# One core, attention and two expert layers: the first expert's first 128 slots are computed while the last token block is still at its gates

## The chip, the cores and the metric

The kernel runs on one core of a Trainium2 chip. The metric is the device time of one execution in microseconds, given as the median of several runs. Engines are named as in the profile: PE (TensorE matmul), PEld (its weight loads), DVE (VectorE), ACT (ScalarE), POOL (GpSimd), and SP, whose queue issues most DMAs. A trace of one execution gives all durations below.

## The reference

Three layers follow one another, on 2304 tokens (4 batches of 576) of 512 features:

```
attn = softmax(top-32 mask(q k^T / 8)) v            # 8 heads of 64, 576 tokens
h    = x @ w_in ; g = h * clip(h + 3, 0, 6) / 6      # w_in [512, 2048]
y    = g @ w_out                                     # w_out [2048, 512]
e    = argmax(y @ w_gate) ; gw = softmax(y @ w_gate)[e]   # 8 experts
out  = gw * (relu(y @ w1[e]) @ w2[e])                # w1 [8, 512, 1024], w2 [8, 1024, 512]
```

Each token passes exactly one of the eight experts. With the given inputs the experts get 328, 333, 249, 289, 285, 189, 284 and 347 tokens; the kernel has room for 384 of each (3 tiles of 128 slots).

## The kernel before, in words

All large products are made of float32r parts: each operand is split into a high part (a rounded copy) and a low part (the rest), and three matmuls (high by high, low by high, high by low) stand for one.

**First layer, in blocks.** The tokens go through the dense layer in 9 blocks of 256 (`NBLK`), each block in 16 steps of 128 hidden features. One step is 12 matmuls of 128x256 into `l1ps` (`l1`, L778), the clipped gate on ACT, DVE and POOL (`epi_a` L784, `epi_b` L790 which writes `gf`, `epi_c` L246 and L798 which write `gh` and `gl`), and 6 matmuls of 128x512 into `yps` (`l2`, L809). `l1ps` has two halves, so the next step but one can't start its first product before DVE has written `gf`. `moe_step` issues a step's pieces, and a scheduler with priorities orders each engine's instructions; what counts below is the order that comes out.

**The gates.** After a block's sixteenth step, `yevac` (L816) copies `yps` to SBUF, and `gate` runs once for each 128 tokens: four transposes, logits (L837), maximum, index and one-hot row (L848 to L860), the place of each token among those of its expert by matmuls with a triangle and with ones (L861, L862), the gate weight (L865), the write of the tokens to `yd` in DRAM (L866, SP) and the scatter of token numbers into the slot table `td` in DRAM (L887, POOL). For blocks 0 to 7 this goes on in the shade of the next block's steps. For the last block there is nothing left to shade it. Its tokens don't go through the table in DRAM: one-hot products add them (`placed`, L1079) to what was read back.

**The slot table.** `load_table` (L903, SP) reads the two tables that blocks 0 to 7 filled, `trow` (L904, DVE) takes the smaller of each pair, `tps` (L1077 to L1079) adds the last block's, and `tabg` (L1080) is the list that the gathers use.

**The experts.** `xgather` fetches the rows of `yd` for one expert (three indirect DMAs of 128 rows, L1092, POOL), `xprep` transposes and splits them (L1101 PE, L1103 ACT, L1104 DVE, and the gate weight `gw` L1105 POOL). Then for each of eight hidden pieces f of the expert come 12 matmuls of 128x384 (`m2l1`, `lp`, L1119), the split of the rectified result (L1123, L1124), and two pieces later 9 matmuls of 128x512 (`m2l2`, `ops`, L1136); `m2out` scales by the gate weight and scatters rows to the output. `wpiece` loads (L916, L919, SP) and splits (L926 ACT, L927 DVE) the expert weights, eight pieces for each expert; six pieces of expert 0 and the first two of expert 1 are split before the last block ends, and expert 0's other two after it.

Of the kernel before, what the change touches and what calls it, by code (L numbers as in the profile page):

```python
# [45 lines left out]
STEP = 400  # L46
# [8 lines left out]
def attention_two_moe_kernel(  # L55
# [139 lines left out]
    def body(cs, exact):  # L195
# [624 lines left out]
        def gate(bk, tt, y):  # L820
            pr("gate")
            i = bk * (TB // P) + tt
            last = bk == NBLK - 1
            yt = (wp[0] if last else m1p).tile([P, NCC, P], F32, tag="yt", bufs=1 + last, name=f"yt{i}")
# [19 lines left out]
            ad = (wp[0] if last else m1p).tile([P, 1], I32, tag="ad", bufs=2, name=f"ad{i}")  # L844
# [28 lines left out]
            if last:  # L873

                ad2 = m1p.tile([P, 1], I32, tag="ad2", bufs=2, name=f"ad2{i}")
                place, in128 = [wp[0].tile([P, n], F32, tag=f"oh{n}", bufs=2, name=f"oh{n}_{i}") for n in (P, NSL)]
                V.tensor_scalar(ad2, ad, P - 1, None, op0=ALU.bitwise_and)
                V.tensor_copy(sc[:, 4:5], ad2)
                V.tensor_tensor(sc[:, 5:6], sc[:, 3:4], sc[:, 4:5], op=ALU.subtract)
                V.tensor_scalar(place, cs["row"], sc[:, 4:5], None, op0=ALU.is_equal)  # L880
                V.tensor_tensor(sc[:, 6:7], cs["tokm"][:, i:i + 1], sc[:, 3:4], op=ALU.subtract)
                V.tensor_scalar(in128, cs["first"].rearrange("p e s -> p (e s)"), sc[:, 5:6], sc[:, 6:7],
                                op0=ALU.is_equal, op1=ALU.mult)
                placed.append((place, in128))

            def to_table():
                G.indirect_dma_start(td[tt], bass.IndirectOffsetOnAxis(ad, 0), tok[:, i:i + 1], None)  # L887

            if last:

                tables.append(to_table)
            else:
                to_table()
            gdone[0] += 1


        NSL = NE * SLOTS
        placed, gdone, trows, tables = [], [0], [], []
# [13 lines left out]
        def wpiece(e, i):  # L912
# [8 lines left out]
            late = kind and pc >= NPC // 2  # L921
            nb = 3 if kind else 5
            pool = tabp[0] if late else wp[0]
            h = pool.tile([P, 4 * FW], F32R, tag=f"wh{kind}", bufs=nb, name=f"wh{e}_{i}")
            l = pool.tile([P, 4 * FW], F32R, tag=f"wl{kind}", bufs=nb, name=f"wl{e}_{i}")
# [9 lines left out]
        def moe_step():  # L935
            g = gpos[0]
            if g >= NG + 3 or (g < NG and blkready[0] <= g // NF1):
                return
            gpos[0] += 1
            if 0 <= g - 1 < NG:  # L940
                epi_a(g - 1)
            yield
            if g >= 3:
                l2(g - 3)
                bk, f = divmod(g - 3, NF1)
                if f == NF1 - 1:
# [108 lines left out]
        pre = []  # L1055
        while gpos[0] < NG + 3 or pend:
            pr0[0] += STEP
            run(moe_step())
            gate_step()
            tc.cur_priority = pr0[0] + STEP  # L1060
            if gdone[0] == NTT - TB // P and not trows:
                load_table()
            if gpos[0] > NG - 12 and len(pre) < NPC + NPC // 2:

                pre.append(2 * len(pre) if len(pre) < NPC else 2 * (len(pre) - NPC) + 1)
                wpiece(0, pre[-1])
        m1.close()
        tc.cur_priority = pr0[0] + 2 * STEP


        tabp[0] = m2.enter_context(tc.tile_pool(name="tabp" + X, bufs=1))
        ps2 = m2.enter_context(tc.tile_pool(name="ps2" + X, bufs=1, space=PSUM))
        tab = tabp[0].tile([P, NSL], I32, name="tab")
        tabg = tabp[0].tile([P, NSL], I32, name="tabg")
        tps = ps2.tile([P, NSL], F32, tag="tp", bufs=2, name="tps")

# [4 lines left out]
        V.tensor_copy(tab, tps)  # L1081

        xst = {}

        def xgather(e):
# [3 lines left out]
            xg = []  # L1089
            for j in range(SLOTS):  # L1090
                x = tabp[0].tile([P, YW], F32, tag="xg", bufs=4, name=f"xg{e}_{j}")
                G.indirect_dma_start(x, None, yd, bass.IndirectOffsetOnAxis(tabg[:, e * SLOTS + j:e * SLOTS + j + 1], 0))  # L1092
                xg.append(x)
# [15 lines left out]
        def m2l1(e, f):  # L1109
# [6 lines left out]
            n = 0  # L1116
            for c in range(NCC):
                for a, b_ in ((h, xh), (h, xl), (l, xh)):
                    PE.matmul(lp, a[:, c, fs], b_[:, c, :], start=(n == 0), stop=(n == 3 * NCC - 1))  # L1119
# [3 lines left out]
            A.activation(hh, lp, AF.Relu)  # L1123
            V.scalar_tensor_tensor(hl, lp, 0.0, r_(hh), op0=ALU.max, op1=ALU.subtract)  # L1124
# [4 lines left out]
        def m2l2(e, f):  # L1129
# [3 lines left out]
            for j in range(SLOTS):  # L1133
# [4 lines left out]
        def m2out(e):  # L1138
            gw = xst[e][2]
            for j in range(SLOTS):  # L1140
                o = tabp[0].tile([P, DM], F32, tag="osb", bufs=3, name=f"osb{e}_{j}")
                A.activation(o, ops_[j], AF.Copy, scale=gw[:, j:j + 1])
                si = G.indirect_dma_start(out, bass.IndirectOffsetOnAxis(tab[:, e * SLOTS + j:e * SLOTS + j + 1], 0), o, None,
                                          bounds_check=NT - 1, oob_is_err=False)
                tc.declare_no_dep(si.ins, group="out" + X, reason="no token is in two slots")
                tc.add_to_no_dep_group("out" + X, si.ins)

        xgather(0)
        for f_ in tables:
            f_()  # L1150
        for i in range(2 * NPC):
            if i not in pre:
                wpiece(0, i)
        for j in range(SLOTS):
            xprep(0, j)
        seq = [(e, f) for e in range(NE) for f in range(NF2)]
        for s in range(len(seq) + 2):
            if s < len(seq):
                e, f = seq[s]
                if e + 1 < NE:  # L1160
                    if f == (e == 0):
# [9 lines left out]
            if s < len(seq) and e + 1 < NE:  # L1171
                wpiece(e + 1, f)
# [111 lines left out]
```

## Time and profile before

| | |
|---|---|
| median of 3 runs | 1294.11 us (1293.91 to 1296.38) |
| the profiled execution's own time | 1292.71 us |
| its span in the trace | 1290.9 us, 1.8 us less than its own time |
| PE busy | 1148.2 us, 89% of the span |
| DVE, ACT, POOL busy | 976.0, 821.9 and 345.8 us |
| mean granted PE clock | 0.957 of full speed |

Durations are taken from the profiled execution; its own time is 1.4 us below the median, so that a time worked out from it has 1.4 us added before it is compared with a median. The stretch that the change touches reaches from about 922 us (the last block's steps) to about 1039 us (the end of the first expert).

### The profile page before, as it was taken

How to read it: one execution, taken by the hardware profiler on the slowest of the kernel's cores; microseconds unless marked ns; L12 is line 12 of the kernel's file. 1: busy time of each engine (PE TensorE's matmuls, PEld its weight loads, DVE VectorE, ACT ScalarE, POOL GpSimd, SP SyncE). 2: the span in 40 equal slices, each digit the busy share in tenths (PEclk: the TensorE clock that was granted, in tenths of full speed). 3: DMA queues.
4: the chain of work that ended last, by engine and by line, in shares of the span. 5: the costliest groups of instructions: out<-in, count | busy, mean ns of one | idle time of the engine just before them, and what ended most of it. 6: DMA issues, size and time to landing. Idle time of an engine off the chain costs nothing.

```text
span 1290.9 us, 23533 instructions
## 1 busy us (share of the span) xinstructions
PE 1148.2 (89%) x7253; PEld 1017.9 (79%) x7253; DVE 976.0 (76%) x3882; ACT 821.9 (64%) x2087; POOL 345.8 (27%) x578
## 2 busy tenths in 40 slices
PE   4465688899999999999999999999975999999995
PEld 3354576788899788888788899898864999999994
DVE  5999999999999998998999999997422444444420
ACT  4777777788777777777777887786412444444421
POOL 2232255332332212222232322222334122212100
PEclk9987579899999999999999999999986999999998
DMA  5444466554644554544434544634774455555400
GB/s 141 134 123 143 119 201 214 162 144 130 151 121 120 137 161 119 153 125 124 119 105 125 158 124 129 147 115 118 265 210 108 142 162 169 164 156 168 133 19 26
DMA packets 184665, 180.21 MB, mean 140 GB/s; under 512 B 123933, under 2 KB 148813, under 8 KB 184528
## 3 DMA queue, kind: packets, MB, share of 16 engines
q1 hardware_dynamic: 180112, 167.52, 45.1%
q0 software_dynamic: 4416, 11.08, 2.9%
q8 instruction: 60, 0.98, 0.3%
q14 instruction: 77, 0.63, 0.2%
HBM read 160.52 MB, written 19.59 MB: 140 GB/s over the span
## 4 chain that ended last, share of the span: by engine, by line
PE 60%; DVE 9%; ACT 4%; DMA 3%; issue 2%; POOL 0%; SPq 0%; POOLq 0%; ACTq 0%; DVEq 0%
PE l1ps L778 11%; PE lp L1119 10%; PE ops L1136 10%; PE yps L809 10%; PE ptps L704 7%; PE sps L556 4%; PE ptps L670 3%; DVE pbuf L654 1%; DVE cd L586 1%; PE ptps L837 1%; DVE z L646 1%; PE tp L1101 1%; DVE z L619 1%; DVE cw L597 1%; PE misc L414 1%
## 5 line engine op out<-in xcount | busy, mean ns | idle before, releaser
L809 PE MATMUL yps<-wo,gh 128*128 128x512 f32 x576 | 209.6, 411 | 1.2 <-DMA wo<-wod 0.8
L778 PE MATMUL l1ps<-xh,wih 128*128 128x256 f32 x576 | 174.6, 303 | 15.2 <-DVE gf L790 10.4
L586 DVE MAX8 cd<-sbuf 128x8 f32<-128x72 f32 x1152 | 182.6, 220 | 2.0 <-ACT sbuf L248 1.9
L246 POOL TENSOR_SCALAR gh<-gf 128x256 fp32r<-128x256 f32 x144 | 64.3, 447 | 391.1 <-DVE gf L790 144.7
L778 PE MATMUL l1ps<-xh,wil 128*128 128x256 f32 x576 | 166.7, 289 | 0.0
L778 PE MATMUL l1ps<-xl,wih 128*128 128x256 f32 x576 | 166.4, 289 | 0.0
L927 DVE TENSOR_TENSOR wl<-raw,wh 128x1024 fp32r<-128x1024 f32 x64 | 79.4, 1243 | 96.3 <-ACT wh L926 94.3
L704 PE MATMUL ptps<-vn,pt 128*128 128x65 f32 (+1 forms) x1152 | 146.6, 282 | 0.0
L704 PEld LDWEIGHTS ptps<-vn,pt 128*128 128x128 f32 x1152 | 143.4, 201 | 0.0
L619 DVE SCALAR_TENSOR_TENSOR z<-sbuf,uall 128x576 f32<-128x576 f32 x144 | 132.7, 922 | 0.4 <-ACT uall L610 0.4
L778 PEld LDWEIGHTS l1ps<-xh,wih 128*128 128x128 f32 x576 | 112.1, 195 | 25.9 <-DVE gf L790 17.5
L654 DVE SCALAR_TENSOR_TENSOR pbuf<-sbuf,tall,pbuf 128x576 f32<-128x576 f32 x144 | 126.2, 877 | 0.1
L926 ACT ACTIVATE wh<-raw 128x1024 fp32r<-128x1024 f32 x64 | 67.7, 1060 | 85.2 <-PE lp L1119 40.3
L809 PEld LDWEIGHTS yps<-wo,gh 128*128 128x128 f32 x576 | 106.8, 191 | 16.9 <-issue 0.9
L784 ACT ACTIVATE gf<-l1ps,three 128x256 f32<-128x256 f32 x144 | 68.3, 474 | 78.4 <-PE l1ps L778 61.3
L670 PE MATMUL ptps<-ident,pbuf 128*128 128x128 f32 x576 | 97.9, 295 | 21.5 <-DVE j L650 14.9
L809 PE MATMUL yps<-wo,gl 128*128 128x512 f32 x288 | 116.3, 404 | 0.8 <-POOL gl L798 0.6
L248 ACT ACTIVATE sbuf<-sps 128x576 f32<-128x576 f32 x144 | 93.1, 647 | 37.2 <-PE sps L556 22.1
L798 POOL TENSOR_TENSOR gl<-gf,gh 128x256 fp32r<-128x256 f32 x144 | 112.5, 782 | 11.4
L627 ACT ACTIVATE pbuf<-sbuf,nb 128x576 f32<-128x576 f32 x144 | 111.2, 776 | 6.8 <-PE ptps L672 2.8
L636 ACT ACTIVATE jk<-sbuf,uall 128x576 bf16<-128x576 f32 x144 | 111.9, 777 | 3.2
L778 PEld LDWEIGHTS l1ps<-xl,wih 128*128 128x128 f32 x576 | 112.2, 195 | 1.8
(178 smaller groups left out, 2932.1 us busy)
## 6 DMA issues: line engine op xcount, KB each, us to landing
wo<-wod SPq DMA_DIRECT2D x144, 512.0 KB
raw<-in_moe_w_dram SPq DMA_DIRECT2D x64, 512.0 KB
vn<-in_v_dram SPq DMA_DIRECT2D x96, 128.0 KB
rawi<-in_moe_w_in_dram SPq DMA_DIRECT2D x16, 512.0 KB
rawo<-in_moe_w_out_dram SPq DMA_DIRECT2D x16, 512.0 KB
qn<-in_q_dram SPq DMA_DIRECT2D x128, 64.0 KB
wod<-wc SPq DMA_DIRECT2D x16, 512.0 KB
yd<-y SPq DMA_DIRECT2D x18, 258.0 KB
```

The costliest lines, as they stand in the source:

```text
L586: V.max(cd[:, c, :], s[:, c * CK:(c + 1) * CK])
L619: V.scalar_tensor_tensor(d["z"], s, d["u"], s, op0=ALU.is_le, op1=ALU.mult)
L627: A.activation(d["p"], d["s"], AF.Exp, bias=d["nb"], scale=SCALE)
L636: A.activation(jk, d["s"][:, 0:S], AF.Sign, bias=ts[t]["u"], scale=-1.0, accum_out=d["sg"])
L654: V.scalar_tensor_tensor(d["p"], d["s"], tall[:, t:t + 1], d["p"], op0=ALU.is_ge, op1=ALU.mult)
L670: PE.transpose(ptps[:, c * P:(c + 1) * P], pb[:, c0 + c * P:c0 + (c + 1) * P], ident)
L704: PE.matmul(d_, a_, b_, start=(i == 0), stop=(i == len(mm) - 1))
L778: PE.matmul(dst, a[:, c, fs], b_[:, c, :], start=(n == 0), stop=(n == 3 * NCC - 1))
L798: G.tensor_tensor(gl, gf, r_(gh), op=ALU.subtract)
L809: PE.matmul(yps[tt], a[:, tsl], b_, start=(f == 0 and m == 0), stop=(f == NF1 - 1 and m == 2))
L1119: PE.matmul(lp, a[:, c, fs], b_[:, c, :], start=(n == 0), stop=(n == 3 * NCC - 1))
L1136: PE.matmul(ops_[j], a[:, js], b_[:, ns], start=(f == 0 and m == 0), stop=(f == NF2 - 1 and m == 2))
```

## The change

**The early tile.** Expert 0's first 128 slots are filled by tokens of blocks 0 to 7 alone if these hold 128 tokens of expert 0. The changed kernel takes that for granted and checks it afterwards: `early_steps` transposes the slot table of blocks 0 to 7 (L1126), takes the token list (L1130, L1131), gathers those rows (`ex`, L1134, POOL) and transposes and splits them (L1139, L1142, L1143; the gate weight `egw` L1146 on POOL), all between steps of the last block. `early_products` runs both expert layers for these 128 slots: for each of eight pieces 12 matmuls of 128x128 (L1163) and 3 of 128x512 (L1176), placed behind the last block's products and among its gates. `early_out` scatters the result. A check (L1222, DVE) compares the early list with the final one and raises the flag that makes the kernel run again in another way; with 328 of the 2304 tokens in expert 0 it doesn't. Expert 0 then has two tiles left: its products are 128x256 instead of 128x384, and 6 instead of 9 of 128x512.

**The last block's gates.** `gate_last` does both halves of the last block at once: `yps` is evacuated on ACT and DVE at the same time (L894, L895), the eight transposes write back into `yps`, two copies (L905, L907) replace four, and `yd` is written in two parts (L898, L927). Its scatters into `td` move behind expert 1's gathers. The gates of other blocks take three pieces per step instead of one.

**The weights.** All eight pieces of expert 0 are loaded and split before the last block ends, and three pieces of expert 1 are loaded then too. Loading (`wload2`) and splitting (`wsplit`) are apart, and one piece is always loaded ahead.

**Expert 1's gathers** are held until the second hidden piece of expert 0 is done, by a copy from `hh` into the gather's tile (L1251).

```diff
+        def gate_last():
...
+            A.activation(ys[0][:, 0:DM], yps[0], AF.Copy, scale=1.0 / 6.0)
+            V.tensor_scalar(ys[1][:, 0:DM], yps[1], 1.0 / 6.0, None, op0=ALU.mult)
+            for tt in range(NTB):
+
+                SP.dma_start(yd[(i0 + tt) * P:(i0 + tt + 1) * P, 0:DM], ys[tt][:, 0:DM])
...
+        def early_steps():
+            tp = misc([P, 2, 2 * P])[:, 0, 0:NSL]
+            PE.matmul(tp, trows[0], ident[0:NSL, 0:NSL], start=True, stop=True)
...
+            x = m1p.tile([P, YW], F32, tag="ysb", bufs=2, name="ex0")
+            G.indirect_dma_start(x, None, yd[0:NT - TB, :], bass.IndirectOffsetOnAxis(tg, 0))
+            yield
+            yield
+            tp = ptps[:, 0:DM].rearrange("p (c n) -> p c n", c=NCC)
+            for c in range(NCC):
+                PE.transpose(tp[:, c, :], x[:, c * P:(c + 1) * P], ident)
...
+            for f in range(NF2 + 2):
+                if f < NF2:
...
+                            PE.matmul(lps[f % 2], a[:, c, fs], b_[:, c, :], start=(n == 0), stop=(n == 3 * NCC - 1))
...
+                if f >= 2:
...
+                        PE.matmul(op, a, b_[:, ns], start=(f2 == 0 and m == 0), stop=(f2 == NF2 - 1 and m == 2))
...
-            gate_step()
+            for _ in range(3):
+                gate_step()
...
-            for j in range(SLOTS):
+                if after is not None:
+
+                    G.tensor_copy(x[:, 0:1], after[:, CAP - 1:CAP])
+                    after = None
...
+            cols = slice(jfirst(e) * P, CAP)
...
-                    if f == (e == 0):
+                    if e == 0 and f == 2:
+                        xgather(1, r_(hst[0, 1][0]))
+                    elif e and f == 0:
                         xgather(e + 1)
```

Three places where the order of instructions changes follow; a number behind a name is a buffer's own and differs between the two kernels.

First DVE, in the last block's steps, where the smaller of the two tables (`trow`) is taken. Before:

```order
L790 SCALAR_TENSOR_TENSOR gf_13873<-gf_13873,l1ps 128x256
L790 SCALAR_TENSOR_TENSOR gf_13908<-gf_13908,l1ps 128x256
L927 TENSOR_TENSOR wl_0_14298<-raw_0_14295,wh_0_14297 128x1024
L790 SCALAR_TENSOR_TENSOR gf_13944<-gf_13944,l1ps 128x256
L869 SCALAR_TENSOR_TENSOR lex_13784,lsc_13783<-ptps,oh_13785 128x8
L872 CAST ad_13786<-lsc_13783 128x1
L790 SCALAR_TENSOR_TENSOR gf_13972<-gf_13972,l1ps 128x256
L927 TENSOR_TENSOR wl_1_14330<-raw_1_14327,wh_1_14329 128x1024
L904 TENSOR_TENSOR trow_14001<-trow_14001,trow_14002 24x128
L790 SCALAR_TENSOR_TENSOR gf_14006<-gf_14006,l1ps 128x256
L790 SCALAR_TENSOR_TENSOR gf_14033<-gf_14033,l1ps 128x256
```

After:

```order
L988 TENSOR_TENSOR wl_3_14047<-raw_3_13990,wh_3_14046 128x1024
L790 SCALAR_TENSOR_TENSOR gf_13795<-gf_13795,l1ps 128x256
L790 SCALAR_TENSOR_TENSOR gf_13829<-gf_13829,l1ps 128x256
L960 TENSOR_TENSOR trow_13784<-trow_13784,trow_13785 24x128
L790 SCALAR_TENSOR_TENSOR gf_13864<-gf_13864,l1ps 128x256
L1130 TENSOR_SCALAR etabg<-misc_13822 128x1
L1131 COPY ewas<-misc_13822 128x1
L988 TENSOR_TENSOR wl_5_14107<-raw_5_14050,wh_5_14106 128x1024
L790 SCALAR_TENSOR_TENSOR gf_13891<-gf_13891,l1ps 128x256
```

Before, the splits of expert 1's first two pieces (`wl_0`, `wl_1`) and the minimum `trow` stand between the block's `gf` results. After, expert 1's splits are not there; `trow` stands five `gf` further up in the block (nine follow it there, four did before), followed by the early list (`etabg`, `ewas`), and splits of expert 0's last pieces (`wl_5`, later `wl_7`) stand between the `gf`.

Second PE, in the last block's sixth and seventh step, where rows of the early tile come in:

```order
L809 MATMUL yps_124<-wo_13803,gl_13840 128x512
L809 MATMUL yps_124<-wo_13803,gh_13839 128x512
L1126 MATMUL misc_13822<-ident,trow_13784 128x24
L809 MATMUL yps_125<-wo_13803,gh_13839 128x512
L809 MATMUL yps_125<-wo_13803,gl_13840 128x512
...
L809 MATMUL yps_125<-wo_13837,gl_13875 128x512
L809 MATMUL yps_125<-wo_13837,gh_13874 128x512
L1139 MATMUL ptps<-ident,ex_13856 128x128 x3
L778 MATMUL l1ps<-xh_136,wih 128x256
L778 MATMUL l1ps<-xl_137,wih 128x256
```

Before, none of the L1126 and L1139 rows is there. The early table's transpose (L1126) now stands in the middle of one step's `yps` products, and the early rows' transposes (L1139) ahead of a step's first `l1ps` product.

Third POOL, from the last block's end to the experts' gathers. Before:

```order
L863 TENSOR_TENSOR ohsum<-ohsum,oh_14149 128x8
L863 TENSOR_TENSOR ohsum<-ohsum,oh_14161 128x8
L887 DMA td_61<-tok,ad_14150 18432x1
L887 DMA td_62<-tok,ad_14162 18432x1
L1092 DMA xg_0_14234<-yd,tabg 128x516
L1092 DMA xg_1_14236<-yd,tabg 128x516
L1092 DMA xg_2_14238<-yd,tabg 128x516
```

After:

```order
L942 TENSOR_TENSOR ohsum<-ohsum,ohl 128x8 x2
L1253 DMA xg_1_14406<-yd,tabg 128x516
L1253 DMA xg_2_14408<-yd,tabg 128x516
L1266 COPY gw_14405<-xg_1_14406 128x1
L1266 COPY gw_14405<-xg_2_14408 128x1
L1236 DMA out_dram<-eo,etab 2304x512
L1251 COPY xg_0_14475<-hh_1_14462 128x1
L1253 DMA xg_1_14478<-yd,tabg 128x516
L1253 DMA xg_0_14475<-yd,tabg 128x516
```

The two scatters into `td` are gone from ahead of expert 0's gathers, of which there are two instead of three. Expert 1's first gather, which stood behind them at once, now waits behind the gate weights, the early output and the copy from `hh_1`. The gather `xg_1` has one new wait that the names don't show: its tile lies where the first layer's pool was, so it waits for PE's last reader of that pool, which is the early tile's last product of its first layer (the last L1163).

## Rows read from the trace of the kernel before

**Rows 1.** The page: the chain that ended last, by engine.

```profile
PE 60%; DVE 9%; ACT 4%; DMA 3%; issue 2%; POOL 0%; SPq 0%; POOLq 0%; ACTq 0%; DVEq 0%
```

**Rows 2.** Stretches of core 0: busy time of each engine, PE clock, DMA share.

```profile
922.00:940.00 18.00, 18.00 (x121) 16.25 (x120) 8.96 (x23) 8.33 (x21) 6.72 (x12) 1.00 0.85 290
...
950.00:960.00 10.00, 6.30 (x37) 5.14 (x37) 3.44 (x7) 2.34 (x5) 3.31 (x5) 1.00 0.46 140
960.00:968.00 8.00, 6.09 (x26) 5.61 (x27) 1.03 (x3) 0.47 (x1) 2.28 (x4) 0.57 0.60 200
...
981.00:993.00 12.00, 2.05 (x10) 1.70 (x11) 5.40 (x29) 2.51 (x5) 7.45 (x9) 0.50 0.53 104
...
1001.00:1039.00 38.00, 38.00 (x198) 34.78 (x197) 16.92 (x21) 15.63 (x23) 3.28 (x5) 0.99 0.46 140
```

**Rows 3.** PE's waits from 920 to 1045: total, times, longest.

```profile
PE tp L1101 <- POOL gw L1105: 8.1, 1, 8.1
PE l1ps L778 <- DVE gf L790: 6.8, 2, 3.9
PE tp L1101 <- DMA xg<-yd,tabg: 2.1, 1, 2.1
```

**Rows 4.** PE's timeline in the last block: start, duration, instruction, idle before.

```profile
951.73 0.39 PE L778 MATMUL l1ps<-xh,wih 128*128 128x256 f32 x1 [2.88 <-DVE gf L790]
...
952.07 0.28 PE L778 MATMUL l1ps<-xh,wil 128*128 128x256 f32 x1
952.18 0.28 PE L778 MATMUL l1ps<-xh,wih 128*128 128x256 f32 x1
...
961.91 0.58 PE L778 MATMUL l1ps<-xh,wih 128*128 128x256 f32 x1 [3.89 <-DVE gf L790]
```

**Rows 5.** Chain of waits from 940 to 1060: start, duration, what.

```profile
940.79 8.22 DMA raw<-in_moe_w_dram
...
952.56 5.36 DMA td<-tok,ad
...
957.94 3.22 DMA trow<-td
...
971.34 4.18 PE yps L809 x18
...
979.34 1.07 PE ptps L837 x8
...
985.26 0.77 issue
986.03 6.56 DMA xg<-yd,tabg
...
993.02 1.10 PE tp L1101 x4
...
999.83 7.03 PE lp L1119 x36
...
1008.95 2.09 PE lp L1119 x12
...
1017.31 0.43 PE tp L1101 x4
...
1036.97 2.08 PE ops L1136 x9
```

**Rows 6.** POOL's timeline: start, duration, instruction, idle before.

```profile
930.35 0.41 POOL L246 TENSOR_SCALAR gh<-gf 128x256 fp32r<-128x256 f32 x1 [1.84 <-PE yps L809]
...
987.34 1.96 POOL L1092 DMA_INDIRECT xg<-yd,tabg  x1 [0.30 <-issue]
...
996.12 0.18 POOL L1105 COPY gw<-xg 128x1 f32<-128x1 f32 x1 [3.30 <-DMA xg<-yd,tabg]
```

**Rows 7.** DVE's timeline at the slot table.

```profile
985.04 0.18 DVE L1080 TENSOR_SCALAR tabg<-tps 128x24 int32<-128x24 f32 x1 [1.18 <-DMA yd<-y]
```

**Rows 8.** Expert gathers at L1092: from issue to landing.

```profile
DMA to landing us min/median/max: 4.0/5.0/8.7
```

More of the change, by code (lines that the diff above doesn't have):

```diff
@@ L872, in gate @@
             V.tensor_copy(ad, sc[:, 3:4])
[L873 to L882, printed above, removed]
+            G.indirect_dma_start(td[tt], bass.IndirectOffsetOnAxis(ad, 0), tok[:, i:i + 1], None)
@@ L910, in body, with wload2 @@
         wst = {}
-        def wpiece(e, i):
+        def wload2(e, i):
             kind, pc = i % 2, i // 2
@@ L920, in wpiece, with wsplit @@
                              w2[e, pc * FW:(pc + 1) * FW, :].rearrange("(j p) n -> p j n", p=P))
[L921 to L925, printed above, removed]
+            return e, i, raw
+        def wsplit(e, i, raw):
+            kind, pc = i % 2, i // 2
+            b_ = (e * NPC + pc) % (6 if kind else 5)
+            pool = wp[0] if b_ < NPC else tabp[0]
+            h = pool.tile([P, 4 * FW], F32R, tag=f"wh{kind}_{b_}", bufs=1, name=f"wh{e}_{i}")
+            l = pool.tile([P, 4 * FW], F32R, tag=f"wl{kind}_{b_}", bufs=1, name=f"wl{e}_{i}")
             A.activation(h, raw, AF.Copy)
@@ L1056, in body, with early_out @@
+        def early_out(x):
+            V.tensor_tensor(es["tab"], es["was"], x[:, DM + 1:DM + 2], op=ALU.add)
+            scatter(es["o"], es["tab"])
+        pre = [2 * i for i in range(NPC)] + [2 * i + 1 for i in range(NPC)]
+        wseq = [(0, i) for i in pre] + [(e, i) for e in range(1, NE) for i in range(2 * NPC)]
+        wraw, n, eg = [], 0, None
         while gpos[0] < NG + 3 or pend:
@@ L1058, in body @@
             run(moe_step())
-            gate_step()
+            for _ in range(3):
+                gate_step()
             tc.cur_priority = pr0[0] + STEP
+            if eg:
+                next(eg, None)
             if gdone[0] == NTT - TB // P and not trows:
                 load_table()
[L1063 to L1067, printed above, removed]
-        tc.cur_priority = pr0[0] + 2 * STEP
[L1071 to L1075, printed above, removed]
+                if early:
+                    eg = early_steps()
+            if n % 2 == 0 and n // 2 <= len(pre):
+                if wraw:
+                    wsplit(*wraw.pop(0))
+                if n // 2 < len(pre):
+                    wraw.append(wload2(*wseq.pop(0)))
+            n += 1
+        assert n > 2 * len(pre) and (not early or "x" in es)
+        for _ in range(3):
+            wraw.append(wload2(*wseq.pop(0)))
+        tc.cur_priority = pr0[0] + 2 * STEP
+        tab = wp[0].tile([P, NSL], I32, name="tab")
+        tabg = wp[0].tile([P, NSL], I32, name="tabg")
+        tps = misc([P, 2, 2 * P])[:, 0, 0:NSL]
         PE.matmul(tps, trows[0], ident[0:NSL, 0:NSL], start=True, stop=False)
@@ L1081, in body, with jfirst, scatter, xgather @@
         V.tensor_copy(tab, tps)
+        if early:
+            V.scalar_tensor_tensor(flag[:, 0:1], tps[:, 0:1], es["was"], flag[:, 0:1], op0=ALU.not_equal, op1=ALU.add)
+            tc.cur_priority += 2 * STEP
+            early_products()
+        m1.close()
+        tabp[0] = m2.enter_context(tc.tile_pool(name="tabp" + X, bufs=1))
+        ps2 = m2.enter_context(tc.tile_pool(name="ps2" + X, bufs=1, space=PSUM))
+        def jfirst(e):
+            return 1 if early and e == 0 else 0
+        def scatter(o, t_):
+            si = G.indirect_dma_start(out, bass.IndirectOffsetOnAxis(t_, 0), o, None, bounds_check=NT - 1, oob_is_err=False)
+            tc.declare_no_dep(si.ins, group="out" + X, reason="no token is in two slots")
+            tc.add_to_no_dep_group("out" + X, si.ins)
         xst = {}
-        def xgather(e):
+        def xgather(e, after=None):
             xh = tabp[0].tile([P, NCC, CAP], F32R, tag="xeh", bufs=2, name=f"xeh{e}")
@@ L1139, in m2out @@
             gw = xst[e][2]
-            for j in range(SLOTS):
+            for j in range(jfirst(e), SLOTS):
                 o = tabp[0].tile([P, DM], F32, tag="osb", bufs=3, name=f"osb{e}_{j}")
                 A.activation(o, ops_[j], AF.Copy, scale=gw[:, j:j + 1])
[L1143 to L1146, printed above, removed]
+                scatter(o, tab[:, e * SLOTS + j:e * SLOTS + j + 1])
         xgather(0)
[L1149 to L1154, printed above, removed]
+        for j in range(jfirst(0), SLOTS):
             xprep(0, j)
@@ L1170, in body @@
                     m2out(e2)
-            if s < len(seq) and e + 1 < NE:
-                wpiece(e + 1, f)
+            if wraw:
+                wsplit(*wraw.pop(0))
+                if wseq:
+                    wraw.append(wload2(*wseq.pop(0)))
+            if s == 3 and early:
+                early_out(xst[0][3][jfirst(0)])
+            if s == 6:
+                for f_ in later:
+                    f_(xst[1][3][SLOTS - 1])
         m2.close()
```

135 lines of the change are left out of this document (116 added, 19 removed).

## The prediction

> **What bounds the kernel now.** I read the chain of waits first, then the table of stretches, then PE's waits and timelines where the change acts. By the chain PE is most of the path [rows 1], so time can be won only where PE stands still or runs slowly, or by giving it less to do. The stretches show where that is: PE is fully busy at full clock from 922 to 940; from 950 to 968 it is busy 12.4 of 18 us and its clock falls to 0.57; from 981 to 993 it is busy 2.05 of 12 us at 0.50; from 1001 it is full again [rows 2]. Its waits name the reasons [rows 3]: 6.8 us for DVE's `gf` in the last block, 8.1 and 2.1 us for the gathers of expert 0. Behind the first lie two stalls, 2.88 us before 951.73 and 3.89 us before 961.91 [rows 4]. The chain shows what was late: a weight load of 8.22 us whose split stood on DVE ahead of a `gf`; then the scatter into the table (5.36 us) and its reading (3.22 us), with `trow` ahead of the next `gf` [rows 5].
>
> Two marks: S, the end of the last block's products at 971.34+4.18 = 975.52, and X, the end of expert 0's last `ops` group at 1036.97+2.08 = 1039.05 [rows 5]. From S to X are 63.5 us.
>
> **Unit prices.** A 128x256 product starts every 0.12 us (952.07 to 952.18, [rows 4]), a 128x384 one every 2.09/12 = 0.174, a 128x512 one every 2.08/9 = 0.231 [rows 5], at full clock. No row has a 128x128 product of this kind. The line through 256 and 384 columns gives 0.066 us; the upper bound is a 128x128 transpose, 0.43/4 = 0.11 [rows 5]. I take 0.066, since the products on that line are of the same kind and load weights of the same size. The Trainium skill ("TensorE: Matmul & The Clock Gate", section "Wait — 56ns, not 53.3ns?") gives 55.6 ns for 128 columns; with it the 73 products below would take 4.1 instead of 4.8 us. No run here shows which holds.
>
> **Term 1, the last block: gain 1.5 us.** Expert 1's splits leave DVE's row there, so the 2.88 goes. `trow` doesn't go, it comes earlier. The gates of block 7 now take three pieces a step, so its second scatter stands behind the fourth `gh` of the last block, which before ran at 930.35 [rows 6]; I estimate its start at 932.4. With the old durations, 5.36 and 3.22, plus `trow` itself, the table is there at about 941.3. PE, undisturbed until then, is at L1126 at about 938.6: a stall of 2.8. The `gf` queued behind `trow` on DVE is late by no more than this. Then the early list goes to POOL, whose gather I put at 6.3 from its release: between 0.77+6.56 [rows 5] and 0.77 plus the median landing of 5.0 [rows 8], since it is alone in its queue. With 0.2 for the list this is 6.5; PE has 9 products of 128x512 and 12 of 128x256 in between (3.5 us) and waits at L1139: 3.0 more. On POOL the copy `egw` waits for the same gather with two `gh` behind it, which PE needs only after L1139. The clock fell in the last block before, when PE stood 3.89 us: a mean of 0.57 from 960 to 968 is 0.50 until 966.9 [rows 2], which costs (966.9-961.9)/2 = 2.5. The two new stalls are shorter each but close together; I take 2.0. Before, the block lost 2.9+3.9+2.5 = 9.3, after 2.8+3.0+2.0 = 7.8: a gain of 1.5. Bounds: with no wait for the table, the early gather landing in 4.0 (0.8+0.2+4.0-3.5 = 1.5) and a full clock the gain is 7.8; with both stalls as long as the longest of before and the clock falling twice, 2x3.9+2x2.5 = 12.8, it is a loss of 3.5. The splits `wl_5` and `wl_7` stand between `gf` too; their loads are issued about 939 to 941 and have landed by 949 even at 8.22, just as PE comes free, so I put nothing on them.
>
> **Term 2, from S to X: gain 2.2 us.** Times from S.
> - *Slot list.* Before, `tabg` starts at 985.04, 9.5 from S [rows 7], after four evacuations and transposes one behind the other (the last logits start at 979.34, [rows 5]). Side by side they save about 1.5: 8.0.
> - *Early products.* By the order 23 of the 96 L1163 and none of the 24 L1176 stand ahead of the list's last row; they fill PE's gaps at no cost. Up to the last L1163 remain 73 x 0.066 = 4.8 and 15 x 0.231 = 3.5. PE's clock was at 0.50 from 981 on [rows 2] with little to do; some of this will run so: 1.7. The last L1163 ends at 18.0 (16.3 with a full clock; at 0.11 each 21.2).
> - *Gather.* This is the point on which the change turns. Expert 0's gathers no longer start with the list but wait for the last L1163. Then 0.77 and 6.56 to the first tile, as before [rows 5], and 1.3 to the second. This is shorter than before, where the pair issued at 987.34 had landed by 996.12 [rows 6], because two rather than four gathers now stand in the queue; the row would be 3.5. The last 9 L1176 (2.1) hide behind it. Transposes 1.10 [rows 5], evacuation 0.8: expert 0's first product at 28.5. Before it was at 24.3 (999.83, [rows 5]). So 4.2 are lost here. The removed scatters' issue on POOL is within the list's term.
> - *Less to do.* Expert 0 loses 8 x (12 x (0.174-0.12) + 3 x 0.231) = 10.7.
> - *Expert 1's gather.* It is held until `hh_1`, about 6.6 after expert 0's first product (24 products partly at half clock, a weight split ahead on ACT). Copy and issue 0.9 and a landing between 5.0 [rows 8] and 6.56 [rows 5] put its first tile at 13.0 after that product, while PE comes to its transposes after four `lp` and two `ops` groups: 48 x 0.12 + 12 x 0.231 = 8.5 plus 1.5 for the slow clock. PE waits 3.0, and I add 1.3 for the clock behind that wait. Before, nothing waited there.
> - Sum: 4.2 - 10.7 + 3.0 + 1.3 = -2.2.
>
> The early scatter, the check and the copies lie on POOL, DVE and ACT behind PE's work. The scatters into `td` that move behind expert 1's gathers serve nobody in this run. From X on nothing changes: weights are split one piece ahead as before or more.
>
> **The sum.** The profiled execution's span 1290.9 - 1.5 - 2.2 = 1287.2; with the 1.8 outside the span 1289.0; the median of the runs lay 1.4 above the profiled execution: 1290.4.
>
> **Rivals.** No-change means within 0.2%, 1291.5 to 1296.7; less than that a measurement here can't tell.
> - *Gathers land fast.* Three gathers now lie in PE's way (early rows, expert 0, expert 1). At 4.0 each [rows 8], they shorten the terms by 1.5, 2.6 and 1.9: 1284.4. The queue is emptier than at 986, when two more gathers followed at once; against it, 6.56 is the one row taken where PE waits. The Trainium skill ("DMA: Bandwidth & Descriptors", section "Anatomy of one DMA — SWDGE (gpsimd) path") puts a transfer from GpSimd's queue at 2.0 us plus its bytes at 436 GB/s; for 258 KB that is an estimate of 2.6 us, and all three would then be shorter still, by some 4 each, near 1281. The row of 6.56 speaks against that rule here. Chance 0.13.
> - *PE keeps its clock* because early products fill the gates: -1.7 on the early products, -0.7 on the transposes, -1.3 behind expert 1's wait, 1286.7. For it speaks that PE has work at once at S; against it, that in the first 8 us this is only 23 short products beside the gate's own, and that the gather leaves PE idle again. Chance 0.10.
> - *A wash*: 128x128 products at 0.11 (+3.2), or the second tile as late as before (+2.2), or both: 1292.6 to 1295.8. The early work then only takes the place of what expert 0 saves. Chance 0.27.
> - *Slower, through gathers that land late.* The three gathers run beside weight loads that are issued more closely than before, with three of expert 1 among them. At 8.7 each [rows 8], the early one costs 3.2 more (0.8+8.7 for 6.3), expert 0's 2.1, expert 1's some 2.5: 7.8 more, 1298.2. It decides from a surplus of 6.3 on, about 8 us for each of the three. For it speaks the DMA share of 0.85 while PE was full [rows 2]; against it, 0.53 at the gathers. Chance 0.17.
> - *No early tile* (the check fires and the kernel runs its second way) would take far longer than any case above; expert 0's 328 tokens of 2304 leave it no chance worth a number.
>
> **Chances and range.** The forecast itself, 1288.2 to 1292.2, has 0.33, of which 0.05 lie above 1291.5. Faster: 0.28+0.13+0.10 = 0.51, rounded up to 0.53 for the fast end of term 1; same 0.30; slower 0.17. The range that leaves out no more than 2 in 10 goes from the fast gathers, 1283.5, to the late ones, 1298.5.
>
> **What would show it right or wrong.** In the changed trace: a PE wait of 2 to 4 us at L1126 and another at L1139, and no `gf` wait of over 1 us in the last block; `tabg` 8 us after the last L809; expert 0's first gather issued just behind the last L1163, some 18 us after it; first L1282 at 28 us; a wait of PE at expert 1's first L1262. If the gather starts with the list instead of the last L1163, the time falls to about 1283; if L1139's wait is over 6 us, the gain of term 1 is gone.

## The result, and the profile after

The changed kernel takes 1305.2 us (median of 4 runs, 1302.64 to 1308.75) against 1294.84 of the kernel before (4 runs); the ratio (not the quotient of the two medians) is 1.0088 with a 95% interval of 1.0067 to 1.0109. It is slower by 0.9%; the forecast was 1290.4, in a range up to 1298.5. The profiled execution took 1302.64, the shortest of the four, 9.9 us above the one before.

The page after: span, PE's busy time, and the chain that ended last by engine.

```profile
span 1300.8 us, 23752 instructions
...
PE 1165.3 (90%) x7352; PEld 1034.3 (80%) x7352; DVE 975.6 (75%) x3891; ACT 819.6 (63%) x2089; POOL 355.5 (27%) x579
...
PE 62%; DVE 7%; ACT 4%; DMA 2%; issue 2%; POOL 1%; SPq 0%; POOLq 0%; ACTq 0%; DVEq 0%
```

PE is busy 17 us more than before, and by the chain it holds 62% of the path where it held 60% [rows 1]: the loss is PE's own time rather than new waiting. The waits of PE from 900 to 1060 (total, times, longest):

```profile
PE misc L1126 <- DVE trow L960: 5.7, 1, 5.7
PE tp L1262 <- DMA xg<-yd,tabg: 2.5, 1, 2.5
PE tp L1262 <- POOL gw L1266: 2.4, 1, 2.4
PE tp L1262 <- ACT eo L1178: 1.3, 1, 1.3
```

The 6.8 us for `gf` and the 8.1 us for expert 0's gather [rows 3] are gone; in their place stand 5.7 us for the table at L1126 and 2.5, 2.4 and 1.3 us at the transposes. Waits alone went down. The chain of waits (start, duration, what):

```profile
936.20 9.08 DMA td<-tok,ad
945.29 2.19 DMA trow<-td
...
973.53 4.20 PE yps L809 x18
...
1003.44 1.30 PE sps L1163 x12
...
1006.83 5.32 DMA xg<-yd,tabg
...
1014.00 5.31 PE lp L1282 x23
...
1045.91 1.40 PE ops L1299 x6
```

With S the end of the last block's products (973.53+4.20 = 977.73, before 975.52 [rows 5]) and X the end of expert 0's last `ops` group (1045.91+1.40 = 1047.31, before 1039.05), the 9.9 us are spread like this:

| part | before | after | difference |
|---|---|---|---|
| first `yps` product of the last block | 921.68 | 924.39 | +2.7 |
| from there to S | 53.8 | 53.3 | -0.5 |
| from S to X | 63.5 | 69.6 | +6.1 |
| from X to the end of the span | 251.9 | 253.5 | +1.6 |

Stretches of PE (busy time, clock, DMA share, GB/s), first before, then after:

```profile
885.00:890.00 5.00, 2.96 (x22) 1.00 0.65 233
890.00:895.00 5.00, 5.00 (x40) 1.00 0.18 69
```

```profile
885.00:890.00 5.00, 2.96 (x20) 0.91 0.64 234
890.00:895.00 5.00, 5.00 (x25) 0.50 0.00 0
...
980.00:990.00 10.00, 9.98 (x55) 0.56 0.02 3
990.00:1000.00 10.00, 10.00 (x46) 0.58 0.00 0
```

The first line pair explains the first part: PE waits 2.0 us just before 890 in both kernels, for the same instruction, and the orders of instructions don't differ there. Behind the wait the clock stayed at 1.00 in the profiled execution of before and fell to 0.50 in that of after. It is a matter of the execution, not of the change: in the profiles of the runs below it fell in some and not in others, and in that of the run without the hold, whose program is the same up to there, it stayed at 1.00. The last lines hold the main finding: from 980 to 1000 PE is fully busy, and its clock is nevertheless 0.56 and 0.58. It is the stretch of the early products. Their spacing (timeline of PE, start and duration):

```profile
987.56 0.41 PE L1163 MATMUL l1ps<-xl,wh 128*128 128x128 f32 x1
987.77 0.41 PE L1163 MATMUL l1ps<-xh,wl 128*128 128x128 f32 x1
...
999.70 0.27 PE L1163 MATMUL sps<-xh,wh 128*128 128x128 f32 x1
999.81 0.28 PE L1163 MATMUL sps<-xl,wh 128*128 128x128 f32 x1
```

A 128x128 product starts 0.21 us after the last one at half clock and 0.11 at full clock. At full clock a 128x256 product took no more than 0.01 longer before [rows 4]. So 96 narrow products, most of them at half clock, ended at 1003.44+1.30 = 1004.74, which is 27.0 us behind S, where 18.0 was forecast. The slot list came 9.6 behind S:

```profile
987.31 0.18 DVE L1219 TENSOR_SCALAR tabg<-misc 128x24 int32<-128x24 f32 x1 [1.17 <-PE misc L1218]
```

### The profile page after: what moved, and what is told of

It is laid out like the page before. It is cut to its first block, busy times and chain, and to the rows that moved or that the text cites. A ratio compares the mean times of both kernels' runs of the same rounds, so it can differ in the third digit from the quotient of the medians.

```text
span 1300.8 us, 23752 instructions
## 1 busy us (share of the span) xinstructions
PE 1165.3 (90%) x7352; PEld 1034.3 (80%) x7352; DVE 975.6 (75%) x3891; ACT 819.6 (63%) x2089; POOL 355.5 (27%) x579
## 4 chain that ended last, share of the span: by engine, by line
PE 62%; DVE 7%; ACT 4%; DMA 2%; issue 2%; POOL 1%; SPq 0%; POOLq 0%; ACTq 0%; DVEq 0%
PE l1ps L778 11%; PE yps L809 10%; PE lp L1282 10%; PE ops L1299 10%; PE ptps L704 8%; PE sps L556 4%; PE ptps L670 3%; DVE pbuf L654 1%; DVE cd L586 1%; PE ptps L836 1%; PE tp L1262 1%; DVE z L646 1%; PE misc L414 1%; DMA td<-tok,ad 1%; DVE z L619 1%
## 5 line engine op out<-in xcount | busy, mean ns | idle before, releaser
L798 POOL TENSOR_TENSOR gl<-gf,gh 128x256 fp32r<-128x256 f32 x144 | 114.3, 794 | 11.3
```

Of the source, the lines that this page charges most:

```text
L798: G.tensor_tensor(gl, gf, r_(gh), op=ALU.subtract)
```

## The experiments

After the result there were two theories. **Price and clock:** the early tile's narrow products take PE as long as wide ones and leave its clock low, so that the early work costs PE more than expert 0 gives back. **Place:** the early work pays, and the waits around it (the gather behind the last L1163, the held gather of expert 1, the table's wait) eat it. Medians and ratios are against the kernel before on the same chip, whose median lay between 1293.2 and 1294.8; runs of different rows were partly taken on different chips, so a difference of two medians can carry an error of about that size.

| run | median us | ratio to before, 95% interval |
|---|---|---|
| no early tile | 1291.6 | 0.9974 (0.9960 to 0.9988) |
| free gathers | 1303.4 | 1.0054 (1.0034 to 1.0074) |
| 256-column early products | 1293.8 | 0.9996 (0.9981 to 1.0011) |
| no hold | 1302.6 | 1.0071 (1.0047 to 1.0096) |
| 256 columns, late table | 1294.9 | 1.0004 (0.9992 to 1.0017) |
| 256 columns, free gathers | 1290.3 | 0.9973 (0.9959 to 0.9988) |
| no early tile, late table | 1292.3 | 0.9988 (0.9971 to 1.0005) |
| 256 columns, late table, free gathers, no hold | 1293.6 | 0.9987 (0.9965 to 1.0008) |
| 256 columns, free gathers, late weights | 1292.2 | 0.9987 (0.9975 to 0.9999) |
| the same and late table | 1284.2 | 0.9941 (0.9918 to 0.9963) |
| no early tile, late weights and table | 1285.8 | 0.9954 (0.9937 to 0.9970) |
| 128 columns, free gathers, late weights and table | 1294.2 | 1.0003 (0.9980 to 1.0026) |

**No early tile.** Every other part of the change stays.

```diff
-        early = not exact
+        early = False
```

> The early tile is left out (no early gather, no L1163 or L1176 products, no check; expert 0 has its three tiles again); the joint gates, the weights split ahead, the held gather of expert 1 and the three gate pieces a step stay. Theory A (price: a 128x128 product costs PE as much as a 128x256 one, 0.213 us at half clock, so that the early tile takes more PE time than expert 0 gives back): 1294 to 1298, 8 or more below the changed kernel. Theory B (place: the early work pays, the waits around it eat it): its gain goes too while the held gather stays, so 1301 or more.

It took 1291.6, on the side of price and clock and 2 us below the range that they had, and below the kernel before: what is left of the change without the early tile is worth some 2 us, and the early tile costs 13.6 in the medians. PE's waits there:

```profile
PE l1ps L778 <- DVE gf L790: 5.2, 1, 5.2
```

The wait in the last block is there without the early tile too (5.2 us, now for `gf`), since `trow` still stands ahead of a `gf` on DVE.

**Free gathers.** Expert 0's gathers get tiles that don't wait for the last L1163.

```diff
-                x = tabp[0].tile([P, YW], F32, tag="xg", bufs=4, name=f"xg{e}_{j}")
+                if e == 0:
+                    x = wp[0].tile([P, YW], F32, name=f"xg{e}_{j}")
+                else:
+                    x = tabp[0].tile([P, YW], F32, tag="xg", bufs=4, name=f"xg{e}_{j}")
```

> Expert 0's two gathers get tiles outside the first layer's pool, so that they start with the slot list (some 18 us earlier) instead of behind the last L1163. Theory A: PE's wait of 4.6 us between the early products and expert 0 goes, and perhaps the clock stays up there: 1300 to 1302, still above the kernel before. Theory B: the late gather is the main cost, 1295 to 1298.

It took 1303.4, above both ranges, and its ten runs lie in two heaps, four at 1296.4 to 1297.9 and six at 1303.3 to 1306.2. Its profile is one of the upper heap. Its stretches of PE:

```profile
980.00:990.00 10.00, 9.98 (x55) 0.57 0.05 14
990.00:1000.00 10.00, 10.00 (x40) 0.50 0.20 53
1000.00:1010.00 10.00, 10.00 (x41) 0.50 0.00 0
```

The clock stayed at half until past 1010, over ten us longer than in the changed kernel, while PE was busy throughout. So what removing the wait saves can't be read from the median: in the profiled execution the clock took it back. That the lower heap is made of executions in which it didn't is likely but not shown, since none of them was profiled. By the median alone, place is not the main cost.

**256-column early products.** The early products of the first layer take the whole buffer of 256 columns; the second half's results aren't used.

```diff
-            es["x"] = xh, xl
+            es["x"] = xbuf[NBLK % 2]
...
-            lps = [l1ps[:, 0, 0:P], sps[:, 0, 0:P]]
+            lps = [l1ps[:, 0, :], sps[:, 0, 0:2 * P]]
```

> The early tile's first-layer products take 256 columns instead of 128 (the second half are old columns of block 7 and their results are not used). Theory A (a 128-column product is bound by something that doesn't shrink with its columns): 0 to 1 us more, 1304 to 1307, start to start 0.213 at half and 0.12 at full clock as for 128 columns; if the clock comes back earlier with fuller products, some us less. Rival (bound by columns): 96 products by 0.053 to 0.107 more, 1310 to 1315.

Twice the columns in 96 products made the kernel 11.4 us faster (1293.8 against 1305.2). That is the expected case of a better clock, and far more of it than the few us that were expected. Stretches and timeline of PE:

```profile
980.00:990.00 10.00, 10.00 (x80) 1.00 0.06 18
990.00:1000.00 10.00, 9.31 (x60) 1.00 0.00 0
```

```profile
985.20 0.28 PE L1163 MATMUL l1ps<-xh,wh 128*128 128x256 f32 x1
985.32 0.28 PE L1163 MATMUL l1ps<-xl,wh 128*128 128x256 f32 x1
```

The clock is 1.00 where it was 0.56 and 0.58, with PE no busier than there. A 256-column product takes 0.12 us, 0.01 more than a narrow one. The last L1163 ends 19.4 behind S instead of 27.0, and these 7.6 us are the whole difference of the two profiled executions (1302.64 and 1295.02). So a narrow product isn't cheaper, and with 256 columns the clock doesn't fall. The edit changes one thing more than the width, though: the order that comes out has 38 of the 96 products, and three of the second layer, ahead of the slot list's last product (L1218), where the changed kernel has 23 and none. Which of the two keeps the clock up, this run alone doesn't say; the last run below comes back to it.

**No hold.** Expert 1's gathers aren't tied to `hh_1`.

```diff
-                    if e == 0 and f == 2:
-                        xgather(1, r_(hst[0, 1][0]))
-                    elif e and f == 0:
+                    if f == (e == 0):
                         xgather(e + 1)
```

> Expert 1's gathers are not held until the second hidden piece of expert 0. If the hold costs what the trace shows (2.4 us of PE's wait and the clock behind it): 1301 to 1303. If the earlier gathers only delay expert 0's second tile in the same queue: no change, 1304 to 1307.

It took 1302.6, in the range of the first expectation, but its runs reach from 1298.8 to 1307.6, over both ranges. PE's wait at expert 1's first transpose is gone from its profile, but there PE ran at half clock until past 1010 (the last L1163 ended 31.0 us behind S):

```profile
990.00:1000.00 10.00, 10.00 (x39) 0.50 0.00 0
1000.00:1010.00 10.00, 9.28 (x30) 0.50 0.16 41
```

With the clock free to change by that much, this run doesn't settle what the hold costs.

**256 columns and a late table.** The table's loads are tied behind the eighth `gf` and its minimum behind the eleventh, by small DVE instructions that read a `gf`.

```diff
+                V.tensor_copy(a_[:, 0:1], gst[gpos[0] - 2][0:NSL, 0:1])
                 SP.dma_start(a_, t_.rearrange("(e s p) o -> e s (p o)", e=NE, p=P)[:, 0:SLOTS, :])
-            V.tensor_tensor(trows[0], trows[0], trows[1], op=ALU.min)
+        def least():
+            z = wp[0].tile([NSL, 1], F32, name="tz")
+            V.tensor_scalar(z, gst[gpos[0] - 2][0:NSL, 0:1], 0.0, None, op0=ALU.mult)
+            V.scalar_tensor_tensor(trows[0], trows[0], z, trows[1], op0=ALU.add, op1=ALU.min)
```

> As the run with 256-column early products (1293.8), and the slot table of blocks 0 to 7 is read and its minimum taken three of the last block's steps later (the loads are tied behind the eighth gf and the minimum behind the eleventh by small DVE instructions). If PE's wait of 5 to 6 us for trow and the slow clock behind it are a cost of their own: 1286 to 1289. Rival (the wait only moves to a later instruction): 1292 to 1295.

1294.9: the wait only moved. The chain of waits names its new end, a weight piece issued at 937.80 that lands 11.39 us later, with its split ahead of a `gf` on DVE:

```profile
937.80 11.39 DMA raw<-in_moe_w_dram
...
949.22 1.06 ACT wh L992
...
950.30 1.22 DVE wl L993
```

**256 columns and free gathers.**

The two edits above together.

> 256-column early products, and expert 0's two gathers in tiles of their own, so that they start with the slot list. If the clock now holds, PE goes from the early products to expert 0 without the 5 us of waiting: 1287 to 1290. Rival (as with narrow products alone, the gather under the early products brings 2 us or nothing): 1291 to 1294.

1290.3, just above the range expected with a clock that holds, and 3.5 us in the medians below the same without free gathers (the intervals of the two just overlap). So place costs something too, once the clock holds. PE's waits:

```profile
PE misc L1126 <- DVE trow L960: 6.2, 1, 6.2
PE tp L1265 <- DMA xg<-yd,tabg: 1.8, 1, 1.8
```

Of the waits at expert 0's transposes 1.8 us are left; the wait for the table, 6.2 us, is now the largest.

**No early tile and a late table.**

```diff
-        early = not exact
+        early = False
...
-            if gdone[0] == NTT - TB // P and not trows:
+            if gpos[0] - 2 == NG - NF1 + 7:
...
+            if gpos[0] - 2 == NG - NF1 + 10:
+                least()
```

> No early tile (as the first experiment, 1291.6), with the table read three steps later. If the trow wait is a cost of its own: 1285 to 1288. Rival (it moves): 1290 to 1293.

1292.3: here too the wait moved (6.1 us for `gf` in its profile) and nothing was won.

**256 columns, late table, free gathers, no hold.**

The run with 256 columns and a late table, with these two edits more:

```diff
+                if e == 0:
+                    x = wp[0].tile([P, YW], F32, name=f"xg{e}_{j}")
...
-                    if e == 0 and f == 2:
-                        xgather(1, r_(hst[0, 1][0]))
-                    elif e and f == 0:
+                    if f == (e == 0):
```

> All four together: 256-column early products, the table three steps later, expert 0's gathers free, expert 1's gathers not held. If the early tile pays once clock and waits are mended, this lies below the run without it and with the late table: 1278 to 1284. If an early tile gives no more PE time back than it takes, it lies at or above that run: 1284 to 1288.

1293.6, above all that was expected. The profile shows the wait in the last block unchanged and a new one, where a transpose waits for DVE's `xel`; it doesn't appear among the waits of the run with free gathers and the hold. What the late table was meant to give didn't come. The run lies 3.3 us above the one with free gathers and the hold; the new wait speaks for the hold as the reason, but no run parts the late table's share from the hold's:

```profile
PE l1ps L778 <- DVE gf L790: 5.9, 1, 5.9
PE tp L1272 <- DVE xel L1275: 4.8, 1, 4.8
```

**256 columns, free gathers, late weights.** The last four weight pieces of expert 0 are loaded one a step from the ninth `gf` on.

```diff
-            if n % 2 == 0 and n // 2 <= len(pre):
-                if wraw:
-                    wsplit(*wraw.pop(0))
-                if n // 2 < len(pre):
-                    wraw.append(wload2(*wseq.pop(0)))
+            if n - 2 in PL:
+                wsplit(*wraw.pop(0))
+            if n in PL:
+                wraw.append(wload2(*wseq.pop(0), tied=gst[gpos[0] - 2] if n > 6 else None))
...
+        PL = (0, 2, 4, 6, 8, 9, 10, 11)
...
+            if tied is not None:
+                V.tensor_copy(raw[:, 0:1], tied[:, 0:1])
```

> As the run with 256-column early products and free gathers of expert 0 (1290.3), and the last four weight pieces of expert 0 are loaded only from the ninth gf of the last block on, one a step (tied by a one-column DVE copy). If the weight loads crowd the scatter into the table and its reading: scatter to table under 7 us instead of 9.1, PE's wait for trow under 4 us instead of 6.2, 1286 to 1288. Rival (other traffic is what makes the table late): the wait stays at 5 to 7 us, 1289 to 1292.

1292.2, just above the rival's range for the time, while the scatter did become shorter as the first theory had it. Chain of waits:

```profile
936.75 5.88 DMA td<-tok,ad
942.64 3.36 DMA trow<-td
```

From the scatter's start to the read table 9.2 us pass, against 11.3 in the changed kernel (9.08+2.19). But the minimum `trow` moved up by one `gf` in this order, so PE needed the table sooner and still waited 5.2 us.

**The same and a late table** (sixth `gf` for the loads, ninth for the minimum).

```diff
-            if gdone[0] == NTT - TB // P and not trows:
+            if gpos[0] - 2 == NG - NF1 + 5:
...
+            if gpos[0] - 2 == NG - NF1 + 8:
+                least()
```

> The same, and the table's loads are tied behind the sixth gf, its minimum behind the ninth, so that no DVE work that waits for a DMA stands ahead of a gf that PE needs. If both kinds of wait are gone: no PE wait over 2 us in the last block, 1282 to 1285. Rival (the wait moves to the next DMA in the row): a wait of 4 us or more remains, 1287 to 1291.

1284.2, in the range of the first theory: 21 us below the changed kernel and 0.59% (interval 0.37 to 0.82%) below the kernel before. Chain, stretches and waits:

```profile
934.07 5.74 DMA td<-tok,ad
```

```profile
940.00:950.00 10.00, 10.00 (x64) 1.00 0.90 261
950.00:960.00 10.00, 9.28 (x59) 1.00 0.99 364
960.00:970.00 10.00, 9.63 (x54) 1.00 0.72 246
970.00:980.00 10.00, 10.00 (x83) 1.00 0.16 55
980.00:990.00 10.00, 9.46 (x67) 1.00 0.18 53
```

```profile
PE tp L1274 <- DMA xg<-yd,tabg: 2.9, 1, 2.9
PE l1ps L778 <- DVE gf L790: 1.1, 2, 0.7
```

The scatter takes as long as in the run before, but nothing on PE asks for it early any more. In the last block PE waits 1.1 us in all, and its clock is 1.00 from 940 to 990.

**No early tile, late weights and table.**

The fastest version without the early tile, and so with expert 0's gathers in their old tiles.

```diff
-        early = not exact
+        early = False
...
-                if e == 0:
-                    x = wp[0].tile([P, YW], F32, name=f"xg{e}_{j}")
-                else:
-                    x = tabp[0].tile([P, YW], F32, tag="xg", bufs=4, name=f"xg{e}_{j}")
+                x = tabp[0].tile([P, YW], F32, tag="xg", bufs=4, name=f"xg{e}_{j}")
```

> No early tile, with the same late pieces and late table. If the waits go: 1284 to 1287, and the difference to the run before it in this list is what the mended early tile is worth (0 to 3 us). Rival (the wait moves): 1289 to 1292.

1285.8. So the last block's waits cost about 6 us by the medians (1291.6 to 1285.8), and less by the ratios (0.9974 to 0.9954, some 3 us). The mended early tile, with its free gathers, is worth 1.6 us in the medians; the intervals of the two overlap, so that its worth isn't settled beyond "0 to some us".

**128 columns, free gathers, late weights and table.** The fastest version with the one difference that the early products are narrow again.

```diff
-            es["x"] = xbuf[NBLK % 2]
+            es["x"] = xh, xl
...
-            lps = [l1ps[:, 0, :], sps[:, 0, 0:2 * P]]
+            lps = [l1ps[:, 0, 0:P], sps[:, 0, 0:P]]
```

> The fastest version so far (1284.2: 256-column early products, free gathers of expert 0, late weight pieces, late table) with the early products' first layer back at 128 columns; nothing else differs. If the narrow products hold PE at half clock wherever they stand: the clock is at 0.50 for 10 us or more behind the last block, 1292 to 1296. Rival (half clock was the after-effect of the last block's stall, which is gone here): 1283 to 1285.

1294.2, ten us above in the medians, with runs from 1285.2 to 1301.3 where the wide version had 1282.2 to 1287.8; the intervals of the two ratios lie apart. The profiled execution is the shortest of the ten: its last block ended 3.3 us earlier than in the wide version's profile, which hides most of the loss in its time. From S to expert 0's first product 32.1 us pass there (966.89 to 998.94), in the wide version 25.0 (970.23 to 995.21). Even in this execution the clock falls behind the last block:

```profile
966.00:972.00 6.00, 5.91 (x44) 1.00 0.24 90
972.00:976.00 4.00, 3.20 (x22) 0.65 0.06 5
976.00:984.00 8.00, 8.00 (x33) 0.50 0.25 66
...
988.00:996.00 8.00, 7.06 (x45) 1.00 0.00 0
```

From 976 to 984 PE is busy all the time at 0.50, with no stall ahead in the last block. So the half clock isn't an after-effect of that block's wait. What made it fall is less clear. The order differs from the wide version's as in the first pair (23 products ahead of the list's last product instead of 38), and PE waited 0.2 and 0.6 us among the gates just before it fell; in the changed kernel it fell without such waits, with PE busy 3.92 of the 4 us from 978 to 982.

That wide rows get the clock back sooner once it has fallen, the changed kernel shows at its stall in the last block:

```profile
940.00:950.00 10.00, 4.33 (x22) 0.86 0.55 137
950.00:960.00 10.00, 10.00 (x57) 0.80 0.80 266
```

The clock fell while PE waited there, and rows of 256 and 512 columns, which begin at 948.01, had it back at 954, after 6 us. The narrow row in the same execution took 17 us, that of the last run 13, and those of the runs without the hold and with free gathers alone hadn't got it back when they ended, 25 and 29 us on.

## Why the prediction was wrong

**Unit price: the step that failed first.** "I take 0.066, since the products on that line are of the same kind and load weights of the same size." The measured spacing is 0.111, the upper bound that I had named and put aside. The line through 256 and 384 columns doesn't go on below 256: each of these products loads weights of its own. The Trainium skill ("TensorE: Matmul & The Clock Gate", section "LDWEIGHTS (loading the stationary operand)") puts a weight load at its columns divided by 1.2, in ns, 107 for 128 columns; the row of 0.111 at full clock agrees with a spacing set by the load, and the figure of 55.6 ns that I had quoted is half of what the rows show. At half clock the rows are 0.21 apart, twice what that section of the Trainium skill gives, and the trace's own records of these loads (PEld) last longer than the spacing, 0.19 us at full and 0.33 at half clock. That the load is the reason is argued here, not shown by a run; that columns aren't is shown by the 256-column run (0.119 for twice the columns). At full clock the 73 products that were left after the list would take 8.1 instead of 4.8 us.

**The clock: the step that failed most.** I had put 1.7 us on half clock behind S and gave 0.10 to a rival in which early products keep the clock up. The opposite came: from about 981 to 998 PE was busy and ran at half clock. Together, price and clock moved the last L1163 from 18.0 to 27.0 behind S. From the list to the last L1163 the sum had 10.0 us, and 17.4 passed (987.31 to 1004.74). An estimate from the rows: the price adds 3.3 of them (8.1 for 4.8), and the 10.8 us at half clock behind the list cost 5.4 where I had 1.7, which adds 3.7; the list itself came 1.6 later. The 256-column run and the last run show that it is the narrow products, together with the order that comes out with them: with 256 columns the clock holds, and 11.4 and 10.0 us come back. That narrow rows stay at the lower clock once it has fallen, and wide ones don't, the rows above show; why it falls, by width or by order, stays open.

**"They fill PE's gaps at no cost."** It was wrong by 1 to 2 us. PE works in its order, and L1163 products stand ahead of gate products: the last L1218 begins 9.1 behind S and the list 9.6, not 8.0, while without the early tile the last L1218 begins 7.5 behind S. Side by side evacuation did save what I had said (without the early tile the list stands 8.0 behind S, as forecast); the early products took it. The list comes 9.4 behind S with 256 columns at full clock too.

**The gather.** The dependence on the last L1163 was right, and so was its size: from the last L1163's end to expert 0's first product 9.3 us (1004.74 to 1014.00) where the sum had 10.5. Expert 0's first product came 36.3 behind S, not 28.5, for the two reasons above. What follows was right: expert 0's share 33.3 us against 32.8 (28.5 of products, 3.0 of wait, 1.3 of clock), with a wait of 2.4 at expert 1's first transpose.

**Term 1, the last block: gain 0.5 instead of 1.5.** PE's wait at L1126 was 5.7, not 2.8, because the scatter took 9.08 instead of 5.36 [rows 5] and began later (936.20 instead of 932.4, of which 2.7 is the block's own later start). At L1139 PE didn't wait at all, where I had 3.0. The two errors nearly cancel, so that the small miss of this term is luck; what is left of it is the slow clock behind the wait, some 3 us (948 to 954) where I had 2.0. That the 2.88 us wait of before would go was right.

**What no term held.** In the profiled execution 2.7 us come from the clock behind the unchanged wait near 890, and 1.6 lie behind X, spread over seven experts and the end; no row shows a cause for these.

**The rivals.** The case that came is on the side I gave 0.17, but by none of my mechanisms: the three gathers landed in 3.4 to 5.3 us, not late. My wash had the right price (0.11) and the wrong sum, because it left the clock as it was.

## What to carry to other kernels

Splitting a tile off a wide product saves PE next to nothing below the width at which the spacing stops falling; take that width from the trace (here 128 columns cost nearly what 256 do) before counting columns, and take the upper of two bounds when the lower one rests on a line drawn past its rows. Work that is meant to fill a gap stands in the same order as what the gap waits for: look at which of the gate's instructions now stand behind it. A wait that ends at a DMA moves to the next DMA in the row when only one instruction is moved; here it went only when table and weights were both put later.

## What the runs showed of the hardware

- A row made mostly of 128x128 float32r products, one behind the other for 17 us, ran at the lower clock (0.50, 1.2 GHz), though PE showed as fully busy; with 256 columns, and in the order that comes out with them, these products ran at 1.00 (2.4 GHz) from their start. The changed kernel, the free-gather run, the run without the hold and the last run show the one, the 256-column runs the other. When a narrow row gets the clock back differs: after 17 and 13 us in the changed kernel and the last run, not within its 25 and 29 us in the other two; rows of 256 and 512 columns had it back after 6 us (948 to 954 in the changed kernel).
- At half clock a 128x128 and a 128x256 product both take 0.21 us; at full clock 0.11 and 0.12. For 256 columns at half clock, PE's timeline of the kernel before, in the last block:

```profile
962.72 0.41 PE L778 MATMUL l1ps<-xh,wih 128*128 128x256 f32 x1
962.93 0.41 PE L778 MATMUL l1ps<-xl,wih 128*128 128x256 f32 x1
```
- A transfer of 512 KB issued in the last block took 11.39 us to land where the DMA share was 0.99 (937 to 949, the run with 256 columns and a late table), and the scatter of 128 token numbers 9.08 us in the changed kernel; in the four runs with late weights, the scatter took 5.7 to 6.5 us.
